# Transposes of 112 rows against transposes of 64 and 48 rows, issued as pairs, in a fused attention and mixer kernel

## The chip, the cores and the metric

The program runs on one core of one Trainium2 chip. The metric is the device time of one launch in microseconds (us); for the kernel before it is the median of three runs, 871.86 us (871.74 to 871.91). The profile is of one further execution of the same program. The engines are called PE (TensorE, the matmuls), PEld (its weight loads), DVE (VectorE), ACT (ScalarE), POOL (GpSimd) and SP (which issues most DMAs).

## The reference, cut to what matters

Three blocks follow one another. All inputs are float32 (the matrices of weights reach the kernel as 64-bit floats and are converted on the chip).

```python
# attention: batch 4, 12 heads, 448 tokens, 64 features to a head
q_n, k_n = rmsnorm(q, g_q), rmsnorm(k, g_k)
attn = softmax(q_n @ k_n.T / 8)                  # 448 x 448 to a head
x = (attn @ v), heads side by side               # (4, 448, 768)
# first mixer: 768 -> 1024, relu, halves u and v
v_n = layernorm(v); v_s = w_spatial @ v_n + b_spatial
x = (u * v_s) @ w_out                            # 512 -> 768
# second mixer: over tokens, then over channels
u = x + relu(x.T @ w_tok1) @ w_tok2 (turned back)
out = u + relu(u @ w_ch1) @ w_ch2
```

## The kernel before, in words

**Tiles.** Two heads are handled together as a pair, 24 pairs in all (NP). The 448 tokens of a pair are cut into four chunks of T = 112 for everything that has tokens on the partitions; P is 128, R is 64, and D, the features of a head, is 64. For each pair q and k are loaded with tokens on the partitions (`load`, line 636), their mean squares are taken (`norms`, line 677: two Square activations on ACT and two row sums on DVE), they are scaled by the roots (`scale`, line 733, on POOL from the third pair on), transposed on PE against an identity matrix so that the features come on the partitions (`transposed`, line 744: four transposes of 112 rows for q, four for k), and copied out of PSUM by ACT, from the ninth pair on with a second half on DVE (line 757 on). `scores` (line 773) multiplies each head of the pair by itself: the contraction is over 64 rows, and the two heads stand in the two halves of the array's rows, so their matmuls are issued two by two. ACT takes the exponentials into a tile `e` of 112 partitions by 2 times 448 columns.

**The turning of the exponentials.** For the product with v the exponentials must have the keys on the partitions. `turned` (line 841) does it for one chunk: seven transposes (ET), each of 112 rows by 128 columns of `e`, the first four into one PSUM bank, the last three into another, and one copy out of each bank, on ACT or (for the second bank of chunks 1 and 3, `ON_DVE`, line 943) on DVE. With 24 pairs and 4 chunks this makes 672 transposes. `values` (line 860) then multiplies with v, 64 output columns to a head, so that the two heads use the two halves of the array's columns. For the first ten pairs (AFTER) the division by the sums is done after that product: `divisors` (line 826) spreads the reciprocals over 64 columns, transposes them (four transposes of 112 rows) and copies the result with one ACT instruction into `over`.

**Order.** Nothing is issued as it is written. Every operation goes into a plan (`Plan.add`, line 159) with a cost from `Plan.estimate` (line 217) and the operations that it depends on, and `place` (line 267) works out an order for every engine: a list schedule by the latest start that a backward pass gives each operation, eight rounds, of which the shortest is kept. For PE the plan holds an attribute `parts`: 0 for a matmul over the whole array, 1 for one of at most 64 rows, 2 for one of at most 64 output columns. Where `parts` changes from one matmul to the next, the plan adds 200 ns (SWITCH, line 346), and it stays with the `parts` that it has while another ready operation of the same `parts` is at most 10,000 ns less urgent (2,500 ns in the first 95 us of plan time; lines 298 to 308, 431). Operations inside `joined_up` (line 211) are issued as one block.

**PSUM.** There are eight banks, of which kind "sc" (scores) owns four, "tp" (transposes) two and "mm" (the mixer's and the values' sums) two (line 133); a kind gets more only where the others' own are not cut into.

**Slots.** `slot` (line 911) lists the work around pair s: loads for s+2, scores of s in four steps, the turning of chunks 2 and 3 of s-1 and 0 and 1 of s, the transposes of q and k of s+1, the values of s-1, the norms of s+2. The mixer's work on the first three batches is merged between the slots and fills PE once the first batch has its six pairs; the fourth batch and the second mixer follow behind.

Of the kernel before, what the change touches and what calls it, by code (L numbers as in the profile page):

```python
# [149 lines left out]
class Plan:  # L150
# [8 lines left out]
    def add(self, engine, fn, args, kwargs):  # L159
# [18 lines left out]
        if engine == "tensor" and fn == "matmul":  # L178
            op.parts = 1 if ins[0].shape[0] <= 64 else 2 if out.shape[0] <= 64 else 0
# [37 lines left out]
    def estimate(self, engine, fn, out, ins, kwargs):  # L217
# [7 lines left out]
        if engine == "tensor":  # L225
            if fn == "transpose":
                return ins[0].shape[0] / 1.2 + 3, 200
# [244 lines left out]
def attention_moe_mixer(  # L472
# [15 lines left out]
    C = 4  # L488
# [137 lines left out]
    class Attention:  # L626
# [9 lines left out]
        def load(self, i):  # L636
            if not 0 <= i < NP:
                return
            b, j = divmod(i, KD)
            t = self.p.tile([T, 2, C, 2, D], F32, tag="raw", bufs=2, name="raw")  # L640

            both = nc.sync if i else nc.scalar

            def load_q(r, on):
                on.dma_start(
                    out=t[:, 0, :, r], in_=q[b, 2 * j + r].rearrange("(c p) d -> p c d", p=T))

            if i:
                load_q(0, nc.sync)
                load_q(1, nc.sync)  # L650
            nc.sync.dma_start(out=t[:, 1, :, 0], in_=k[b, 2 * j].rearrange("(c p) d -> p c d", p=T))

            src = k[b, 2 * j + 1]
            both.dma_start(out=t[:R, 1, 0, 1], in_=src[LAST:])
            both.dma_start(out=t[R:, 1, 0, 1], in_=src[:T - R])
            nc.sync.dma_start(
                out=t[:, 1, 1:, 1], in_=src[T - R:LAST].rearrange("(c p) d -> p c d", p=T))
            if not i:
                load_q(0, nc.sync)
                load_q(1, nc.sync)  # L660
            self.raw[i] = t
            if i == 2:
                self.third = t.tile

# [12 lines left out]
        def norms(self, i, wait=()):  # L677
            if not 0 <= i < NP:
                return
            p, n = self.p, 4 * C  # L680
            raw = self.raw[i].rearrange("p a c r d -> p (a c r) d")
            ss = p.tile([P, n], F32, tag="ss", bufs=3, name="ss")
            for h in (slice(0, n // 2), slice(n // 2, n)):
                sq = p.tile([T, n // 2, D], F32, tag="sq", bufs=1, name="sq")
                sq.tile.after = list(sq.tile.after) + list(wait)
                nc.scalar.activation(sq, raw[:, h], AF.Square)
                nc.vector.reduce_sum(ss[:T, h], sq, axis=AX.X)
            r = rsqrt(p, ss[:T], T, n, 1.0 / D, "r", bufs=3, on=nc.gpsimd if i > 1 else nc.vector)
            self.r[i] = [r[:, :n // 2], r[:, n // 2:]]

        def first(self):
# [3 lines left out]
            raw = self.raw[0].rearrange("p a c r d -> p a (c r) d")  # L695
            self.r[0] = [None, None]

            def squares(a, on):
                sq = p.tile([T, 2, S], F32, tag="e", bufs=EB, name="e").rearrange("p r s -> p (r s)")
                sq = sq[:, :n * D].rearrange("p (n d) -> p n d", d=D)  # L700
                if on is nc.scalar:
                    on.activation(sq, raw[:, a], AF.Square)
                else:
                    on.tensor_tensor(sq, raw[:, a], raw[:, a], op=ALU.mult)
# [15 lines left out]
            self.transposed(0, 0, [known])  # L720
            self.warm(WARM2, [op for _, op in self.qt[0].tile.writers])
            self.transposed(0, 1)
# [10 lines left out]
        def scale(self, i):  # L733
# [4 lines left out]
            for a in range(2) if i else (1,):  # L738
                on = nc.gpsimd if i > 1 else nc.vector
                raw = self.raw[i][:, a].rearrange("p c r d -> p (c r) d")  # L740
                roots = self.r[i][a][:T]
                on.tensor_tensor(raw, raw, roots.unsqueeze(2).to_broadcast([T, 2 * C, D]), op=ALU.mult)

        def transposed(self, i, a, wait=()):
            if not 0 <= i < NP:
                return
            tp = psum.tile([P, C, T], "tp", "tp")
            for c in range(C):
                nc.tensor.transpose(
                    tp[:, c, :], self.raw[i][:, a, c].rearrange("p r d -> p (r d)"), ident[:T, :T])  # L750
            tpf = tp.rearrange("p c t -> p (c t)")
            if i < WHOLE:
                to = self.qt if a == 0 else self.kt
                t = to[i] = self.p.tile([P, S], F32, tag="qt" if a == 0 else "kt", name="whole")
                t.tile.after = list(t.tile.after) + list(wait)
                nc.scalar.activation(t, tpf, AF.Copy, scale=1.0 if a == 0 else self.gg[:, 0:1])
                if a:
# [784 lines left out]
```

## Time and profile before

| what | value |
|---|---|
| median of three runs | 871.86 us |
| span of the profiled execution | 870.8 us |
| time around the span, by the median | 1.06 us |
| PE busy | 854.8 us, 98% |
| DVE, ACT, POOL busy | 684.0, 534.0, 407.9 us |
| the chain that ended last, on PE | 92% |

A line of the profile names an engine, an operation, the tiles that it writes and reads (out<-in) with their partitions and elements, how many there were (x), busy time and the mean of one. In the list in order of time a line merges neighbouring instructions of one kind: start, time from the first one's start to the last one's end, count. A matmul's time has its latency in it, so neighbouring lines overlap, and the pace of a group is read from starts. A transposing matmul stands as `tp<-ident,e 112*128 112x112`: 112 rows by 128 columns are loaded as weights, and the 112 columns of the identity are streamed through them.

### The profile page before, as it was taken

To read this page: it belongs to the slowest core of one execution; us is meant where nothing else is said; L and a number is where in the kernel's file an instruction comes from. 1 tells how busy PE (TensorE), PEld (TensorE's weight loads), DVE (VectorE), ACT (ScalarE), POOL (GpSimd) and SP (SyncE) were. 2 spreads that over 40 slices of the span, in tenths; PEclk is the share of its full clock that TensorE was granted. 3 is DMA by queue.
4 is the path that set the end of the run, shared out by engine and by line. 5 is a ranking of instruction groups with operands and counts; after the bars stand their busy time and mean duration, and the time that the engine had idled before them with its cause. 6 is when DMAs were issued, how large, how long until landed. Compare 5 with 4: busy or idle time off the path is not lost.

```text
span 870.8 us, 15419 instructions
## 1 busy us (share of the span) xinstructions
PE 854.8 (98%) x5000; PEld 721.8 (83%) x5000; DVE 684.0 (79%) x1343; ACT 534.0 (61%) x1278; POOL 407.9 (47%) x538
## 2 busy tenths in 40 slices
PE   6999999999999999999999999999999999999998
PEld 5554567777687787777889999999999999999997
DVE  6889999877886767867476466989889986998963
ACT  6999988788686767766453356655335654343331
POOL 2554746786667636464235223234233108415560
PEclk9999999999999999999999999999999999999999
DMA  7655665467545467444777567876564745752441
GB/s 167 180 134 150 188 182 167 131 198 235 168 120 157 135 198 209 118 144 113 228 260 243 179 219 264 254 238 211 160 164 137 242 123 170 224 167 58 145 153 64
DMA packets 153263, 152.27 MB, mean 175 GB/s; under 512 B 77152, under 2 KB 136352, under 8 KB 153184
## 3 DMA queue, kind: packets, MB, share of 16 engines
q1 hardware_dynamic: 152720, 151.26, 58.7%
q8 instruction: 40, 0.66, 0.3%
q14 instruction: 39, 0.32, 0.1%
q10 hardware_dynamic: 464, 0.03, 0.0%
HBM read 112.44 MB, written 38.80 MB: 174 GB/s over the span
## 4 chain that ended last, share of the span: by engine, by line
PE 92%; ACT 4%; DMA 3%; DVE 1%; issue 0%; SPq 0%; ACTq 0%; POOL 0%; DVEq 0%; POOLq 0%
PE h2ps L424 18%; PE o_ps L424 18%; PE tp L424 10%; PE av L424 8%; PE vps L424 7%; PE ups L424 7%; PE sc L424 7%; PE xps L424 7%; PE sps L424 4%; PE u_ps L424 4%; PE h1ps L424 3%; ACT e L424 2%; DMA raw<-in_moe_w_in_dram 1%; DMA wo<-wo_d 1%; ACT et L424 1%; DMA vrest<-in_v_dram 0%
## 5 line engine op out<-in xcount | busy, mean ns | idle before, releaser
L424 PE MATMUL h2ps<-op,w 128*128 128x448 f32 x756 | 154.2, 366 | 0.0
L424 PE MATMUL o_ps<-w,op 128*128 128x384 f32 x882 | 153.1, 334 | 0.0
L424 PEld LDWEIGHTS o_ps<-w,op 128*128 128x128 f32 x882 | 152.9, 188 | 0.0
L424 PEld LDWEIGHTS h2ps<-op,w 128*128 128x128 f32 x756 | 141.7, 188 | 11.2
L424 ACT ACTIVATE e<-sc,nm 112x448 f32<-112x448 f32 x184 | 119.6, 673 | 24.4 <-DVE nm L424 24.1
L424 DVE TENSOR_REDUCE nm<-sc 112x1 f32<-112x448 f32 x192 | 109.4, 614 | 11.7 <-PE sc L424 11.3
L424 POOL TENSOR_TENSOR src<-src 128x384 f32<-128x384 f32 x48 | 59.2, 1243 | 76.0 <-DMA src<-c_d 62.7
L424 PEld LDWEIGHTS tp<-ident,e 112*128 112x128 f32 x672 | 74.3, 142 | 23.2 <-issue 6.4
L424 ACT ACTIVATE op<-c 128x768 fp32r<-128x768 f32 x49 | 41.5, 847 | 83.6 <-PE o_ps L424 80.2
L424 POOL TENSOR_SCALAR e<-e,sums 112x448 f32<-112x448 f32 x112 | 71.5, 656 | 42.3 <-DVE sums L424 17.1
L424 PE MATMUL tp<-ident,e 112*128 112x112 f32 x672 | 87.5, 263 | 0.4 <-ACT e L424 0.4
L424 ACT ACTIVATE et<-tp 128x448 f32<-128x448 f32 (+1 forms) x144 | 72.6, 544 | 11.7 <-PE tp L424 11.2
L424 DVE SCALAR_TENSOR_TENSOR word<-raw,word 128x256 uint32<-128x256 uint32 (+2 forms) x132 | 70.7, 536 | 1.7
L424 POOL TENSOR_TENSOR u<-u,o 128x384 f32<-128x384 f32 x28 | 41.0, 1483 | 65.7 <-ACT o L424 35.4
L424 DVE TENSOR_SCALAR word<-word 128x256 f32<-128x256 f32 (+5 forms) x132 | 56.7, 437 | 16.9 <-ACT word L424 16.1
L424 DVE TENSOR_TENSOR op<-c,op 128x768 fp32r<-128x768 f32 x49 | 58.7, 1198 | 9.9 <-ACT op L424 9.9
L424 PE MATMUL ups<-xp,wu 128*128 128x448 f32 x288 | 66.1, 373 | 0.0
L424 PE MATMUL av<-et,v 128*64 128x448 f32 x288 | 60.3, 549 | 1.5 <-ACT et L424 1.5
L424 PE MATMUL xps<-wo,g 128*128 128x384 f32 x288 | 59.7, 346 | 1.1 <-DMA wo<-wo_d 1.1
L424 PE MATMUL vps<-wv,xp 128*128 128x512 f32 x216 | 59.2, 408 | 0.0
L424 PEld LDWEIGHTS ups<-xp,wu 128*128 128x128 f32 x288 | 52.6, 188 | 5.0 <-ACT et L424 0.3
L424 DVE TENSOR_TENSOR c<-c,h2ps 128x448 f32<-128x448 f32 x84 | 49.9, 613 | 8.6 <-PE h2ps L424 8.4
(149 smaller groups left out, 1666.5 us busy)
## 6 DMA issues: line engine op xcount, KB each, us to landing
src<-c_d SPq DMA_DIRECT2D x132, 192.0 KB, 3.0
wu<-wu_d SPq DMA_DIRECT2D x16, 768.0 KB, 4.9
wo<-wo_d SPq DMA_DIRECT2D x16, 768.0 KB, 4.8
raw<-in_moe_w_ch_dram SPq DMA_DIRECT2D x36, 256.0 KB, 3.5
raw<-in_moe_w_ch_dram SPq DMA_DIRECT2D x24, 384.0 KB, 3.7
raw<-in_q_dram SPq DMA_DIRECT2D x48, 112.0 KB, 2.8
u<-u_d SPq DMA_DIRECT2D x28, 192.0 KB, 3.9
out_dram<-u SPq DMA_DIRECT2D x28, 192.0 KB, 1.9
```

What stands on the lines that cost most here:

```text
L424: getattr(getattr(self.nc, op.engine), fn)(*args, **kwargs)
```

## The change

The transposes of `e`, of q and k, and of the spread reciprocals are done with at most 64 rows each. A transpose of 112 rows by 128 columns becomes two, one of rows 0 to 63 and one of rows 64 to 111, with 64 and 48 columns of the identity streamed, into two PSUM banks; the two are issued next to each other, and all of a chunk (seven times two) are issued as one block. Copies out of PSUM take a bank each, now split by rows: 7 times 64 and 7 times 48 columns instead of 4 times 112 and 3 times 112. For `over` there are two copies where there was one.

q and k of a pair share one tile of 128 partitions: q has its tokens, 64 at a time, on the lower half, k on the upper, in G = 7 chunks. So `norms` works on 448 columns where it had 512, `scale` has pieces of 512 and 384 where it had two of 512, and there are seven times two transposes where there were eight. The loads of q and k of a pair are five DMAs instead of six. The first pair keeps its old form in two tiles of the `e` ring (`load_first`, `transposed_first`). `parts` is now worked out for transposes as well, and the plan costs a transpose of at most 64 rows at 28 ns.

```diff
-        if engine == "tensor" and fn == "matmul":
+        if engine == "tensor":
             op.parts = 1 if ins[0].shape[0] <= 64 else 2 if out.shape[0] <= 64 else 0
...
             if fn == "transpose":
+                if ins[0].shape[0] <= 64:
+                    return 28, 200
                 return ins[0].shape[0] / 1.2 + 3, 200
...
+            t = self.raw[i] = self.p.tile([P, G, 2, D], F32, tag="raw", bufs=2, name="raw")
+            for r in range(2):
+                nc.sync.dma_start(out=t[:R, :, r], in_=q[b, 2 * j + r].rearrange("(c p) d -> p c d", p=R))
+            nc.sync.dma_start(out=t[R:, :, 0], in_=k[b, 2 * j].rearrange("(c p) d -> p c d", p=R))
             src = k[b, 2 * j + 1]
+            nc.sync.dma_start(out=t[R:, 0, 1], in_=src[LAST:])
+            nc.sync.dma_start(out=t[R:, 1:, 1], in_=src[:LAST].rearrange("(c p) d -> p c d", p=R))
...
+            for cs in (slice(0, G // 2 + 1), slice(G // 2 + 1, G)):
                 on = nc.gpsimd if i > 1 else nc.vector
...
+            tps = [psum.tile([P, G, R], "tp", "tp") for _ in range(2)]
+            raw = self.raw.pop(i).rearrange("p c r d -> p c (r d)")
+            with nc.joined_up():
+                for c in range(G):
+                    for a in range(2):
+                        me = slice(a * R, (a + 1) * R)
+                        nc.tensor.transpose(tps[a][:, c], raw[me, c], ident[me, me])
+            for a in range(2):
+                self.kept(i, a, tps[a].rearrange("p c t -> p (c t)"))
...
-            over = self.over[i] = p.tile([P, S], F32, tag="over", bufs=1, name="over")
-            nc.scalar.activation(over, tp.rearrange("p c t -> p (c t)"), AF.Copy)
+            over = self.over[i] = p.tile([P, C, T], F32, tag="over", bufs=1, name="over")
+            for tp, (t, m) in zip(tps, HALVES):
+                nc.scalar.activation(over[:, :, t:t + m], tp, AF.Copy)
...
-            for h, tiles in enumerate((range(C), range(C, ET))):
-                tp = psum.tile([P, C, T], "tp", "tp")
-                for n in tiles:
-                    t = n // 2 * P + n % 2 * (S + R)
-                    nc.tensor.transpose(tp[:, n - tiles[0], :], e[:, t:t + P], ident[:T, :T])
-                et = self.et[i][:, tiles[0]:tiles[-1] + 1, c * T:(c + 1) * T]
-                tpf = tp[:, :len(tiles)]
+            tps = [psum.tile([P, ET, m], "tp", "tp") for _, m in HALVES]
+            with nc.joined_up():
+                for n in range(ET):
+                    at0 = n // 2 * P + n % 2 * (S + R)
+                    for tp, (t, m) in zip(tps, HALVES):
+                        nc.tensor.transpose(tp[:, n], e[t:t + m, at0:at0 + P], ident[t:t + m, t:t + m])
+            for h, (t, m) in enumerate(HALVES):
+                et = self.et[i][:, :, c * T + t:c * T + t + m]
...
             self.turned(s - 1, 3)
-            self.transposed(s + 1, 0)
+            self.transposed(s + 1)
             yield
             self.scores(s, 1)
             self.normalise(s, 0)
-            self.transposed(s + 1, 1)
             self.values(s - 1)
...
+    G = S // R
+    HALVES = (0, R), (R, T - R)
```

## Rows read from the trace of the kernel before

**Rows 1.** The page: engines over the span, and the chain that ended last.
```profile
PE 854.8 (98%) x5000; PEld 721.8 (83%) x5000; DVE 684.0 (79%) x1343; ACT 534.0 (61%) x1278; POOL 407.9 (47%) x538
...
PE 92%; ACT 4%; DMA 3%; DVE 1%; issue 0%; SPq 0%; ACTq 0%; POOL 0%; DVEq 0%; POOLq 0%
```
**Rows 2.** Busy time by stage: stretch and its length, PE, PEld, DVE, ACT, POOL, clock.
```profile
20.00:100.00 80.00, 76.99 (x461) 41.04 (x459) 70.62 (x157) 77.21 (x220) 45.73 (x74) 0.97 0.60 162
100.00:160.00 60.00, 60.00 (x375) 45.20 (x374) 54.95 (x136) 51.11 (x140) 35.90 (x55) 1.00 0.59 168
160.00:300.00 140.00, 140.00 (x908) 107.06 (x907) 108.78 (x254) 108.01 (x301) 100.30 (x161) 1.00 0.57 165
300.00:436.00 136.00, 136.00 (x858) 106.02 (x857) 91.90 (x236) 89.58 (x240) 66.87 (x108) 1.00 0.58 169
```
**Rows 3.** PE's groups between 100 and 436 us, by shape.
```profile
L424 PE MATMUL tp<-ident,e 112*128 112x112 f32 x504 | 65.2, 259 | 0.0
...
L424 PE MATMUL tp<-ident,raw 112*128 112x112 f32 x128 | 16.0, 260 | 0.0
...
L424 PE MATMUL tp<-ident,wide 112*128 112x112 f32 x16 | 2.2, 262 | 0.0
```
**Rows 4.** PE in order of time: start, time, operation, count.
```profile
123.32 1.07 PE L424 MATMUL vps<-wv,xp 128*128 128x512 f32 x4
124.23 0.83 PE L424 MATMUL tp<-ident,e 112*128 112x112 f32 x7
124.99 1.47 PE L424 MATMUL sc<-kt,qt 64*112 64x448 f32 x12
126.40 2.48 PE L424 MATMUL av<-et,v 128*64 128x448 f32 x12
128.70 0.92 PE L424 MATMUL av<-et,vrest 128*64 128x448 f32 x4
129.55 1.48 PE L424 MATMUL sc<-kt,qt 64*112 64x448 f32 x12
130.97 0.98 PE L424 MATMUL tp<-ident,raw 112*128 112x112 f32 x8
131.72 3.02 PE L424 MATMUL vps<-wv,xr 128*128 128x512 f32 x12
134.58 0.83 PE L424 MATMUL tp<-ident,e 112*128 112x112 f32 x7
135.19 1.47 PE L424 MATMUL ups<-xp,wu 128*128 128x448 f32 x6
136.50 0.83 PE L424 MATMUL tp<-ident,e 112*128 112x112 f32 x7
...
152.30 0.46 PE L424 MATMUL sc<-kt,qt 64*112 64x448 f32 x2
```
**Rows 5.** PE in order of time: two runs of transposes, 112 and 128 columns streamed.
```profile
196.86 1.50 PE L424 MATMUL tp<-ident,e 112*128 112x112 f32 x14
...
511.88 0.82 PE L424 MATMUL tp<-ident,x 128*128 128x128 f32 x6
```
**Rows 6.** PE's group of transposes with 128 columns, whole span.
```profile
L424 PE MATMUL tp<-ident,x 128*128 128x128 f32 x96 | 16.0, 272 | 0.0
```
**Rows 7.** Weight loads in order of time: transposes, a first and its successor; scores.
```profile
156.10 0.14 PEld L424 LDWEIGHTS tp<-ident,e 112*128 112x128 f32 x1 [0.18 <-ACT e L424]
...
156.16 0.24 PEld L424 LDWEIGHTS tp<-ident,e 112*128 112x128 f32 x2
...
152.30 0.17 PEld L424 LDWEIGHTS sc<-kt,qt 64*112 64x112 f32 x2 [0.70 <-DVE wpart L424]
```
**Rows 8.** Copies out of PSUM and work on q and k, by shape, whole span.
```profile
L424 ACT ACTIVATE et<-tp 128x448 f32<-128x448 f32 x96 | 55.2, 577 | 10.9 <-PE tp L424 10.5
...
L424 ACT ACTIVATE sq<-raw 112x512 f32<-112x512 f32 x46 | 30.8, 670 | 0.6 <-DVE ss L424 0.6
L424 ACT ACTIVATE et<-tp 128x336 f32<-128x336 f32 x48 | 23.0, 479 | 0.8 <-PE tp L424 0.7
...
L424 DVE TENSOR_REDUCE nm<-sc 112x1 f32<-112x448 f32 x192 | 109.4, 614 | 11.7 <-PE sc L424 11.3
L424 DVE TENSOR_REDUCE ss<-sq 112x8 f32<-112x512 f32 x46 | 31.3, 680 | 12.1 <-ACT sq L424 12.0
L424 DVE COPY et<-tp 128x336 f32<-128x336 f32 x48 | 24.1, 501 | 22.4 <-PE tp L424 22.3
...
L424 POOL TENSOR_TENSOR raw<-raw,ry 112x512 f32<-112x512 f32 x44 | 47.0, 1083 | 1.3
```
**Rows 9.** DMA issues for q and k: count, KB each, us to landing.
```profile
raw<-in_q_dram SPq DMA_DIRECT2D x48, 112.0 KB, 2.8
...
raw<-in_k_dram SPq DMA_DIRECT2D x24, 84.0 KB, 2.8
...
raw<-in_k_dram SPq DMA_DIRECT2D x23, 12.0 KB, 2.4
```

More of the change, by code (lines that the diff above doesn't have):

```diff
@@ L701, in squares @@
                 if on is nc.scalar:
-                    on.activation(sq, raw[:, a], AF.Square)
+                    on.activation(sq, raw[a], AF.Square)
                 else:
-                    on.tensor_tensor(sq, raw[:, a], raw[:, a], op=ALU.mult)
+                    on.tensor_tensor(sq, raw[a], raw[a], op=ALU.mult)
                 return sq
@@ L735, in scale, with transposed, transposed_first @@
                 return
-            for a in range(2) if i else (1,):
-                on = nc.gpsimd if i > 1 else nc.vector
[L740 to L744, printed above, removed]
+            if not i:
+                raw = self.raw[i][1].rearrange("p c r d -> p (c r) d")
+                roots = self.r[i][1][:T]
+                nc.vector.tensor_tensor(raw, raw, roots.unsqueeze(2).to_broadcast([T, 2 * C, D]), op=ALU.mult)
+                return
+            for cs in (slice(0, G // 2 + 1), slice(G // 2 + 1, G)):
+                on = nc.gpsimd if i > 1 else nc.vector
+                n = 2 * (cs.stop - cs.start)
+                raw = self.raw[i][:, cs].rearrange("p c r d -> p (c r) d")
+                roots = self.r[i][:, 2 * cs.start:2 * cs.stop]
+                on.tensor_tensor(raw, raw, roots.unsqueeze(2).to_broadcast([P, n, D]), op=ALU.mult)
+        def transposed(self, i):
             if not 0 <= i < NP:
                 return
+            tps = [psum.tile([P, G, R], "tp", "tp") for _ in range(2)]
[7 more added lines that the diff above has]
+                self.kept(i, a, tps[a].rearrange("p c t -> p (c t)"))
+            self.r.pop(i)
+        def transposed_first(self, a, wait=()):
             tp = psum.tile([P, C, T], "tp", "tp")
@@ L749, in transposed, with kept @@
                 nc.tensor.transpose(
-                    tp[:, c, :], self.raw[i][:, a, c].rearrange("p r d -> p (r d)"), ident[:T, :T])
-            tpf = tp.rearrange("p c t -> p (c t)")
+                    tp[:, c, :], self.raw[0][a][:, c].rearrange("p r d -> p (r d)"), ident[:T, :T])
+            self.kept(0, a, tp.rearrange("p c t -> p (c t)"), wait)
+            if a:
+                self.raw.pop(0)
+        def kept(self, i, a, tpf, wait=()):
+            to = self.kt if a else self.qt
@@ L877, in values @@
             if i < AFTER:
-                over = self.over.pop(i)
+                over = self.over.pop(i).rearrange("p c t -> p (c t)")
                 nc.vector.tensor_tensor(over, av[:, :S], over, op=ALU.mult)
```

88 lines of the change are left out of this document (39 added, 49 removed).

## The prediction

> **What bounds the kernel now.** I read the page first: PE is busy for 98% of the span and makes 92% of the chain that ended last, where DVE is busy for 79% and ACT for 61% [rows 1]. A busy PE need not be an engine at its limit, so the busy times by stage come next [rows 2]. From 100 to 436 us, where attention and the first mixer run side by side, PE has no idle time at all; DVE comes nearest in the first 60 us of it (55 of 60) and falls to two thirds later, ACT falls from 51 of 60 to 90 of 136. There PE's work is the time. From 20 to 100 us it is otherwise: the mixer has nothing ready, and ACT is busy for 77.2 of 80 us. At most 2.8 us can come out of that stretch, whatever PE saves. After 436 us the transposes that the change touches are over.
>
> So the question is what PE's transposes cost between 100 and 436 us. The groups by shape [rows 3] give 504 of `e`, 128 of q and k, 16 of the reciprocals. At 28 of `e` to a pair these are 18 pairs' work. Their mean of 259 ns is latency; the pace is read from a run of fourteen that takes 1.50 us [rows 5]: (1.50 - 0.259) / 13 = 95.5 ns. A run of six with 128 columns streamed gives (0.82 - 0.272) / 5 = 110 ns [rows 5, 6]. Both are 0.85 to 0.86 ns a column, so the streamed columns set the pace, not the rows.
>
> **What a pair of halves costs.** No row shows a transpose of 64 rows, so it is bounded. Streaming 64 columns takes 64 x 0.853 = 55 ns, and the partner's 48 columns less, if the two run beside each other. The second limit is the weight load, still 128 columns: where nothing held it up, a second load began 0.06 us after the first [rows 7]. If a half's load goes beside its partner's, a pair costs 60 ns, if the loads take turns 120 ns; if only the streams take turns, (64 + 48) x 0.853 = 95.5 ns, as now. The nearest rows are those of the scores, which already run two halves of the rows: two loads lie together in 0.17 us [rows 7], and twelve matmuls of 64 rows take 1.47 us, as do six over the whole array with as many columns each [rows 4]. Both loads and streams run beside each other there. I take 60 ns, and keep 55 and 120.
>
> Then, between 100 and 436 us: for `e` 504 x (95.5 - 60) = 17.9 us; for q and k 128 x 95.5 - 112 x 60 = 5.5 us, seven pairs taking the place of eight transposes; for the reciprocals 16 x 35.5 = 0.6 us. Together 24.0 us off PE, or 1.33 us a pair of heads.
>
> **What it adds on PE: changes between halves and whole.** In the list in order of time [rows 4] a visit to the scores and values has four changes (scores, values, scores, mixer), and a change is visible as a gap: twelve scores have a pace of (1.47 - 0.46) / 5 = 0.20 us a pair, so six pairs need 1.21 us, but the next kind starts 1.41 us after them. A change costs 0.2 us; the plan's SWITCH has the same. The transposes work over the whole array now and are strewn between mixer matmuls at no such price (124.23, 134.58, 136.50). Afterwards each block of transposes that stands alone between mixer matmuls pays two changes, 0.4 us, and saves only 7 x 35.5 = 0.25 us. A block next to scores pays nothing.
>
> The plan knows this and holds on to the kind of work it has. How many blocks can it bring next to scores? A block fills both of the transposes' banks. They are free again when two copies are done: 577 and 479 ns on ACT, or 501 ns on DVE beside ACT's [rows 8], so 0.6 to 1.1 us and the hops, behind whatever ACT has before them. Two blocks in a row would make PE wait; a block, two chunks of scores (1.4 us) and another block would not. A visit of the present form has four such places around its two runs of scores, one for each chunk of `e`. The fifth block, q and k, finds none and costs a visit of its own; and since exponentials come two chunks at a time and five `e` buffers hold them back, I add half a visit for a chunk that isn't ready. One and a half further visits for each of 18 pairs, at 0.4 us, are 10.8 us. The ends: none, and three (21.6 us).
>
> **The rest.** ACT: from the copies, 112 columns are (577 - 479) = 98 ns, 0.88 ns each, with some 185 ns fixed [rows 8]. The second copy of `over` adds 0.19 us for the first ten pairs; squares of 448 in place of 512 columns save 2 x 0.06 us a pair. DVE saves 2 x (680 - 614) = 0.13 us a pair on the sums, POOL a quarter of one scaling of 1083 ns, 0.27 us [rows 8]. These lie beside PE from 100 us on and are costed at nothing there; if PE's cover goes, they are the gain. ACT's copies of `et` have 448 and 336 columns as before, in shorter runs; nothing to a third more is possible, and from 100 us on ACT has room (51 of 60 is the tightest). The first copy now waits until all fourteen halves are done, 7 x 60 = 0.42 us after the block begins where four transposes took 0.38, so nothing is late by it. q's transposes wait for both scalings, up to 1.1 us later than now, in a slot of 336 / 18 = 18.7 us that prepares them one slot ahead: nothing. SP issues five loads where it issued six, the sixth of 2.4 us to landing [rows 9]; the same bytes now go to 64 partitions. The loads run two slots ahead, which covers even a doubling of 2.8 us. Nothing is queued longer on SP.
>
> In the stretch from 20 to 100 us scores, turning and scores alternate, so PE gains more there than anywhere, but ACT is the limit and gets 0.07 us a pair more work. Of the 2.8 us I take 1.0, with ends 0 and 2.8.
>
> **Sum.** 24.0 + 1.0 - 10.8 = 14.2 us. The profiled span is 870.8 us and the median 871.86, so 1.06 us lie around it; I leave them. 871.86 - 14.2 = 857.7 us.
>
> **Rivals.**
>
> *The halves don't keep that pace.* A pair is two loads and two matmuls, four instructions in 60 ns; the scores show four in 0.2 us [rows 4] and no row shows them closer together. If PE starts them no faster than streams in turn would run, a pair costs 95.5 ns, the 24.0 us are gone and the changes stay: 871.9 + 10.8 = 883 us. With loads in turn it is 632 pairs x 120 = 75.8 us against 648 x 95.5 = 61.9: another 13.9 us, 897. For it: nothing shows such a rate. Against it: the concurrency that the scores show. Chance 0.11.
>
> The Trainium skill, TensorE: Matmul & The Clock Gate, section "Wait — 56ns, not 53.3ns?", says that matmuls start at least about 25 ns apart however few their columns are, and the page TensorEngine Tiling (Array Packing), "Instruction Overhead", warns against dividing a dimension that is small already. Two matmuls at that figure are 50 ns and would leave my 60; if it held for the loads too, four would be 100 ns, and the sum would come out as in the rival above. No row here shows which.
>
> *The blocks don't find their places.* This ends slower without any fault of the halves: the place is the change of `parts` around each block, the price 0.4 us, and the two banks are why. If all five blocks of a pair stand alone, 5 x 0.4 = 2.0 us are paid for 1.33: 18 x 0.67 = 12 us slower, 884 us. It decides from 1.33 / 0.4 = 3.3 further visits a pair. For it: today's blocks mostly stand alone [rows 4]. Against: the plan costed them at no change then; now it charges 200 ns each. Chance 0.08.
>
> *Another engine takes over.* The blocks wait for visits, so `e` buffers come free later, scores and exponentials later, and PE meets gaps where it had mixer work; or DVE, at 55 of 60, is the limit from 100 to 160 us. Then some 14 us turn into waits: 871 to 872 us. Against it: PE has no gap now, and DVE's work shrinks too. Chance 0.07.
>
> **How the numbers follow.** The forecast has 0.74, its own range 845 (no further visit, all of the early 2.8) to 868 us (three further visits: 24.0 - 21.6 + 1); pairs at 55 ns would give 3 us more, 842. The range from 843 to 874 holds it and the rival of no change, and leaves out the two slow ones with 0.19. A difference of 0.2%, 1.7 us, is about what a measurement of this kernel can tell from none. Faster 0.74, same 0.07, slower 0.19.
>
> **What would show it.** In the profile after: a block of fourteen halves between two starts at about 0.42 us plus latency, halves of a pair starting together, loads too; transposes next to scores in the order of PE, and some four to seven changes a pair of heads instead of four; PE still without gaps from 100 us on and the end of attention near 422 us instead of 436; ACT as full as now before 100 us. Wrong would be a pace of 95 ns or more for a pair, blocks alone between mixer matmuls five times a pair, or PE waiting for `et` copies.

## The result, and the profile after

The kernel after takes 881.38 us (median of four runs, 880.90 to 883.16), the kernel before beside it 871.80 us: a ratio of 1.011 with an interval of 1.0095 to 1.0124. It is slower by 9.6 us; the prediction said 14.2 us faster, and 881.4 us lies outside its range. The page of the profile after, the engines' shares and the chain that ended last, against [rows 1]:

```profile
PE 843.5 (96%) x5850; PEld 706.5 (80%) x5850; DVE 681.4 (77%) x1343; ACT 533.3 (61%) x1288; POOL 403.5 (46%) x538
...
PE 77%; ACT 10%; DVE 5%; DMA 4%; issue 2%; SPq 2%; POOL 1%; ACTq 0%; DVEq 0%; POOLq 0%
```

PE is busy 11.3 us less than in [rows 1], so work did come off it. But span less busy time, PE's idle time, rose from 870.8 - 854.8 = 16.0 to 881.4 - 843.5 = 37.9 us, and the chain lost its 92% on PE: a tenth of it now runs over ACT. The stages, against [rows 2] (same columns), tell where:

```profile
20.00:100.00 80.00, 65.29 (x609) 35.71 (x609) 67.07 (x144) 70.46 (x202) 41.80 (x70) 0.86 0.57 155
100.00:160.00 60.00, 54.52 (x426) 33.57 (x425) 47.25 (x121) 47.15 (x139) 28.37 (x47) 0.89 0.45 128
160.00:300.00 140.00, 138.44 (x1216) 104.78 (x1217) 110.91 (x264) 110.59 (x309) 98.75 (x162) 1.00 0.61 174
300.00:436.00 136.00, 134.46 (x1155) 105.07 (x1152) 99.21 (x243) 95.32 (x260) 73.85 (x121) 1.00 0.53 156
```

From 160 us on PE is nearly full, as before. Between 20 and 160 us it now idles 20.2 us where it idled 3.0, and ACT, whose 77.2 of 80 us set the pace of the first stage, is at 70.5. No engine is full there any more: they wait for each other. The granted clock, third from the right, is 0.86 and 0.89 where it was 0.97 and 1.00.

When the values of a pair (`av`) start, read off PE in order of time, shows the two effects apart:

| start of, us | before | after | later by |
|---|---|---|---|
| values of the 1st pair | 30.7 | 34.0 | 3.3 |
| values of the 8th pair | 126.4 | 148.5 | 22.1 |
| first mixer matmul of the values (`vps`) | 100.5 | 116.4 | 15.9 |
| values of the 24th pair | 428.1 | 438.6 | 10.5 |

22 us are lost up to the eighth pair, and 301.7 - 290.1 = 11.6 us come back over the other sixteen. What comes back is the forecast's mechanism; what is lost is a stretch that the forecast had costed as a small gain.

**What came as forecast.** PE in order of time, around one visit to scores and values of the kernel after:

```profile
204.83 2.48 PE L426 MATMUL av<-et,v 128*64 128x448 f32 x12
207.14 0.92 PE L426 MATMUL av<-et,vrest 128*64 128x448 f32 x4
207.99 0.64 PE L426 MATMUL tp<-ident,e 64*128 64x64 f32 x14
208.45 1.45 PE L426 MATMUL sc<-kt,qt 64*112 64x448 f32 x12
209.74 0.59 PE L426 MATMUL tp<-ident,e 64*128 64x64 f32 x14
210.25 5.50 PE L426 MATMUL xps<-wo,g 128*128 128x384 f32 x30
```

The block of seven pairs at 209.74 us lasts 0.59 us with a latency of some 0.225 us (the groups below), so a pair takes (0.59 - 0.225) / 6 = 61 ns; the block at 207.99 us, 0.64 us long, gives 69. That is close to the 60 ns that were taken, where a whole transpose had 95.5 [rows 5]. Blocks stand on both sides of the scores, as the plan wanted. PE's groups of the transposes of `e` between 100 and 436 us, against [rows 3]:

```profile
L426 PE MATMUL tp<-ident,e 64*128 64x64 f32 x519 | 46.5, 227 | 0.2 <-ACT over L426 0.2
L426 PE MATMUL tp<-ident,e 48*128 48x48 f32 x519 | 44.9, 225 | 2.2 <-DVE et L426 1.3 <-ACT et L426 0.8
```

The changes of `parts`, counted in the order of PE, rose from 37 to 54 between 160 and 300 us and from 28 to 48 between 300 and 436: by 17 in 7.5 slots and 20 in 7.3, some 2.5 a pair of heads, 1.2 visits where 1.5 were costed.

**What did not.** Between 20 and 130 us, PE's costliest waits before (one line) and after, and the transposes' own wait for copies, that is for a bank, in the view of the waits (engine, what waited, for what; us in total, times, longest):

```profile
PE av L424 <- ACT et L424: 1.5, 3, 0.7
```
```profile
PE tp L426 <- ACT e L426: 9.3, 8, 7.6
PE av L426 <- ACT et L426: 7.4, 5, 2.6
PE av L426 <- ACT e L426: 1.8, 1, 1.8
...
PE tp L426 <- ACT et L426: 1.0, 3, 0.5
```

The same stretch on ACT, before and after:

```profile
ACT et L424 <- PE tp L424: 1.7, 3, 1.2
...
ACT xp L424 <- DVE over L424: 0.5, 2, 0.3
```
```profile
ACT et L426 <- PE tp L426: 5.6, 4, 2.6
ACT xp L426 <- DVE over L426: 4.6, 2, 3.2
```

One wait of the first line after, 7.6 us, is the start, told of below; it began ahead of 20 us, and the kernel before has 4.96 us there. The rest is the circle that follows: the values wait for the copies of the turned exponentials, those copies for the blocks, the blocks for the exponentials, and each engine is idle in turn. The last line closes the circle: `over` is the values' product times the reciprocals, made on DVE, so ACT, which has `xp` to copy from it ahead of its next exponentials, stands waiting for the values themselves, 4.6 us where it was 0.5. One turn of the circle in order of time, PE first (from the values of the pair before, with two blocks in a row at 82.38 us and four later values behind it), then ACT; the time in brackets is the wait ahead:

```profile
60.48 2.48 PE L426 MATMUL av<-et,v 128*64 128x448 f32 x12 [1.75 <-ACT e L426]
...
70.39 0.64 PE L426 MATMUL tp<-ident,e 48*128 48x48 f32 x13 [0.17 <-ACT e L426]
...
71.62 0.65 PE L426 MATMUL tp<-ident,raw 64*128 64x64 f32 x13 [0.33 <-ACT e L426]
74.06 4.75 PE L426 MATMUL av<-et,v 128*64 128x448 f32 x12 [1.79 <-ACT et L426]
...
82.38 1.04 PE L426 MATMUL tp<-ident,e 64*128 64x64 f32 x28
...
92.58 3.60 PE L426 MATMUL av<-et,v 128*64 128x448 f32 x12 [2.65 <-ACT et L426]
...
108.33 4.75 PE L426 MATMUL av<-et,v 128*64 128x448 f32 x12 [1.77 <-ACT et L426]
...
127.70 4.17 PE L426 MATMUL av<-et,v 128*64 128x448 f32 x12 [0.75 <-ACT et L426]
...
148.55 4.07 PE L426 MATMUL av<-et,v 128*64 128x448 f32 x12 [1.45 <-ACT et L426]
```
```profile
71.41 0.94 ACT L426 ACTIVATE et<-tp 128x448 f32<-128x448 f32 x2
72.16 0.71 ACT L426 ACTIVATE e<-sc,nm 112x448 f32<-112x448 f32 x1
...
72.77 0.71 ACT L426 ACTIVATE e<-sc,nm 112x448 f32<-112x448 f32 x1
...
73.38 0.63 ACT L426 ACTIVATE et<-tp 128x448 f32<-128x448 f32 x1
```

PE is through with the blocks by 72.3 us, but the last copy stands behind two more exponentials on ACT and ends at 74.0; the values begin then. They also take 4.75 us for twelve, and the later ones 3.60 to 4.75, where the undisturbed ones at 204.83 took 2.48. The granted clock was lower there (busy times by stretch, columns as in [rows 2], kernel after):

```profile
18.70:28.90 10.20, 6.62 (x60) 4.42 (x62) 7.69 (x20) 8.31 (x24) 6.36 (x12) 0.50 0.54 113
73.30:80.10 6.80, 6.04 (x18) 2.15 (x20) 4.09 (x10) 4.61 (x13) 2.24 (x4) 0.50 0.66 177
```

There, and in five more stretches up to 152 us (from 46.0, 93.8, 107.4, 127.9 and 148.4 us on), TensorE runs at 1.2 instead of 2.4 GHz, 37.5 us in all. The five from 73.3 us on each lie within 1.3 us of the start of values that had waited for `et`, the five of the fence. The kernel before has one such stretch ahead of its last microsecond or two:

```profile
17.75:24.60 6.85, 5.56 (x24) 4.00 (x25) 5.20 (x13) 5.82 (x17) 2.91 (x6) 0.50 0.59 137
```

**The start.** SP's queue, before and after:

```profile
6.54 1.38 SPq L424 DMA_DIRECT2D raw<-in_moe_w_in_dram  x3
10.17 0.89 SPq L424 DMA_DIRECT2D raw<-in_q_dram  x2
```
```profile
7.28 1.27 SPq L426 DMA_DIRECT2D raw<-in_q_dram  x2
8.60 1.97 SPq L426 DMA_DIRECT2D raw<-in_k_dram  x3
10.61 1.06 SPq L426 DMA_DIRECT2D raw<-in_moe_w_in_dram  x2
```

The first pair's q and k now lie in the ring of `e`, so both `raw` buffers are free for the second and third pair, and SP issues the third pair's loads at 7.28 us, ahead of the mixer's weights; before, they went out at 10.17, behind them. ACT stands in front of the first exponential until the weights land:

```profile
12.70 0.67 ACT L424 ACTIVATE word<-raw 128x512 f32<-128x512 f32 x1 [0.62 <-DMA raw<-in_moe_w_in_dram]
13.27 0.71 ACT L424 ACTIVATE e<-sc,nm,r0y 112x448 f32<-112x448 f32 x1
```
```profile
15.91 0.66 ACT L426 ACTIVATE word<-raw 128x512 f32<-128x512 f32 x1 [2.91 <-DMA raw<-in_moe_w_in_dram]
16.48 0.71 ACT L426 ACTIVATE e<-sc,nm,r0y 112x448 f32<-112x448 f32 x1
```

That is 3.2 us, and the first values are late by 3.3.

So three theories stand beside each other for the 22 us: the **start** (order of the loads), the **form** (fourteen halves in one block that holds both banks, with both copies behind its end), and the **clock**.

Two more things go with them. The form also changes what the values wait for: a values matmul reads one turned tile over all 448 tokens, so with copies split by rows it needs both copies of every chunk, where the first half of a pair's values needed only the copies of the first bank. And every kernel below has a new **plan**, worked out anew for all engines. What a plan alone moves can be read off `e_only8` (last group), which leaves loads and forms of the first eight pairs as they were: its first values start at 33.4 us, its seventh pair's at 113.6 and its eighth's at 135.5, against 30.7, 110.1 and 126.4 in the kernel before (twelve scores and eight transposes more lie ahead of the last, some 2 us of its 9.1 by [rows 4], an estimate). So differences of some 5 us between two single plans are not proof of a cause by themselves.

### The profile page after: what moved, and what is told of

The parts are those of the page before. It is cut to its first block, busy times and chain, and to the rows that moved or that the text cites. A ratio compares the mean times of both kernels' runs of the same rounds, so it can differ in the third digit from the quotient of the medians.

```text
span 881.4 us, 17062 instructions
## 1 busy us (share of the span) xinstructions
PE 843.5 (96%) x5850; PEld 706.5 (80%) x5850; DVE 681.4 (77%) x1343; ACT 533.3 (61%) x1288; POOL 403.5 (46%) x538
## 4 chain that ended last, share of the span: by engine, by line
PE 77%; ACT 10%; DVE 5%; DMA 4%; issue 2%; SPq 2%; POOL 1%; ACTq 0%; DVEq 0%; POOLq 0%
PE o_ps L426 17%; PE h2ps L426 17%; PE av L426 8%; PE xps L426 7%; PE ups L426 6%; PE tp L426 5%; PE sc L426 4%; PE vps L426 4%; PE sps L426 4%; ACT e L426 4%; PE h1ps L426 3%; PE u_ps L426 2%; ACT et L426 2%; SPq L426 2%; DMA raw<-in_k_dram 1%
## 5 line engine op out<-in xcount | busy, mean ns | idle before, releaser
L426 PEld LDWEIGHTS h2ps<-op,w 128*128 128x128 f32 x756 | 141.7, 188 | 11.7 <-DVE op L426 0.8
L426 ACT ACTIVATE e<-sc,nm 112x448 f32<-112x448 f32 x184 | 117.3, 655 | 9.2 <-DVE nm L426 8.8
L426 POOL TENSOR_TENSOR src<-src 128x384 f32<-128x384 f32 x48 | 61.2, 1283 | 74.3 <-DMA src<-c_d 41.8
L426 POOL TENSOR_SCALAR e<-e,sums 112x448 f32<-112x448 f32 x112 | 72.2, 661 | 31.8 <-DVE sums L426 22.3
L426 ACT ACTIVATE et<-tp 128x448 f32<-128x448 f32 x144 | 69.6, 525 | 23.3 <-PE tp L426 22.9
L426 PEld LDWEIGHTS tp<-ident,e 64*128 64x128 f32 (+1 forms) x1344 | 54.4, 140 | 35.6 <-issue 10.7
L426 PE MATMUL av<-et,v 128*64 128x448 f32 x288 | 69.9, 627 | 11.4 <-ACT et L426 9.5
L426 DVE SCALAR_TENSOR_TENSOR word<-raw,word 128x256 uint32<-128x256 uint32 (+2 forms) x132 | 77.7, 589 | 1.9
L426 PE MATMUL tp<-ident,e 48*128 48x48 f32 (+1 forms) x1344 | 62.6, 228 | 3.5 <-DVE et L426 1.3
L426 DVE TENSOR_SCALAR word<-word 128x256 uint32<-128x256 uint32 (+5 forms) x132 | 54.3, 417 | 11.9 <-ACT word L426 9.8
L426 PE MATMUL xps<-wo,g 128*128 128x384 f32 x288 | 55.7, 341 | 0.1
L426 PEld LDWEIGHTS av<-et,v 128*64 128x64 f32 x288 | 21.4, 153 | 42.4 <-issue 29.2
```

The source lines that it names most:

```text
L426: getattr(getattr(self.nc, op.engine), fn)(*args, **kwargs)
```

## The experiments

All times are medians beside the kernel before on the same chip (872.0 to 872.4 us). "Time at 1.2 GHz" is worked out from the mean granted clock c of a run's span, 2 x (1 - c) x span, as a mean over the runs; by this the kernel before has 7 us and the one after 39.

**third: the old place of the third pair's loads in the queue.**

```diff
+            if i == 2:
+                t.tile.after = [u for x in self.pair0 for u in x.tile.users]
...
+            self.pair0 = tq, tk
```

> The changed kernel, with one wait put back: the load of q and k of the third pair waits until the first pair's q and k have been transposed, as it did when the first pair took one of the two raw buffers. Theory start: the loss before 20 us (first exponentials at 16.5 us in place of 13.3, behind an ACT wait of 2.9 us for the load of w_in, which SP now issues behind the third pair's loads) comes from that; first exponentials back at 13.3 us and 3 us off the time, 878 us. Theories clock and order (below) alone: the start comes back, but the time stays at 880 to 882 us, since the loss up to 150 us is made elsewhere.

Measured 874.70 us (872.21 to 876.70, ten runs; ratio 1.0026, 1.0012 to 1.0039): 6.7 us faster than after, more than either theory had. But the first exponential came only 0.85 us sooner, for the weights still landed late:

```profile
14.97 0.66 ACT L426 ACTIVATE word<-raw 128x512 f32<-128x512 f32 x1 [2.10 <-DMA raw<-in_moe_w_in_dram]
...
15.63 0.71 ACT L426 ACTIVATE e<-sc,nm,r0y 112x448 f32<-112x448 f32 x1
```

The other 5.8 us are not the wait itself. The plan is worked out anew with the added dependence, and the time at 1.2 GHz fell to 27.6 us; how much each has of it stays open. The later experiments keep this edit, unless they say otherwise.

**fill: keep PE busy in its waits.** To the kernel after, matmuls of the identity by itself are added on PE, eight ahead of the first eight pairs' values and three ahead of each of their blocks; the plan doesn't know of them.

```diff
+            if i < FILL:
+                nc.fill[nc.ops[-1]] = tps[0].rearrange("p n m -> p (n m)")[:, :P], ident, 3
...
+                if i < FILL and not kc:
+                    nc.fill[nc.ops[-1]] = av[:, :P], ident, 8
```

> The changed kernel with the same plan and order, plus idle work for PE: for the first eight pairs eight matmuls of the identity with itself are issued just before the first values matmul, and three before each block of halves of e, into the bank that the block then overwrites. Nothing else differs. Theory clock: PE does so little in the first 150 us that its clock is granted at 1.2 GHz in seven stretches (31 us more than before), and the values, which everything waits for, run at half pace (4.8 us in place of 3.16): the fillers keep the clock at 2.4 GHz, the values take 3.2 us, and 9 to 13 us come off: 868 to 872 us. Theory order: the loss is waits that the new order of blocks makes, and the clock only shows them; the clock may rise, but the time stays at 879 us or more, and the fillers cost up to 3 us.

891.73 us (ratio 1.0227, 1.0210 to 1.0244), far above what either theory gave. The clock held (0.96 and 1.00 in the first two stages of the table by stage, against 0.86 and 0.89); the filling is the likely trouble. PE in order of time:

```profile
49.94 2.05 PE L425 MATMUL av<-ident 128*128 128x128 f32 x16
...
55.08 0.94 PE L425 MATMUL tp<-ident 128*128 128x128 f32 x6
```

One filling matmul is two instructions here (eight show as sixteen), so eight cost 2.0 us and three 0.87, some 5.5 us a pair, and they ran where PE had no wait as well. It tells that a full clock alone doesn't bring the time back if it must be bought with PE's time, and no more.

**third_fill4: the same, cheaper.** `third` with four such matmuls ahead of the first eight pairs' values alone.

> The kernel with the third pair's load waiting (third), with four matmuls of the identity issued just before the first values matmul of the first eight pairs, into the bank that the values overwrite; about 1 us a pair, where PE now waits 0.4 to 2.0 us for copies. Plan and order are the same. Theory clock: the clock no longer falls in those waits, values take 3.2 us throughout, and the time falls to 867 to 872 us. Theory order: 874 to 878 us whatever the clock does.

871.26 us (869.63 to 877.21, ten runs; 0.9999, 0.9983 to 1.0014), 18.3 us at 1.2 GHz in place of 27.6. So 9.3 us less of the low clock go with 3.4 us less time, 0.37 us for each, net of the filling. Between the runs of one kernel time goes with the clock too: of the eleven kernels with six to ten runs, nine have slopes of 0.23 to 0.52 us for 1 us at 1.2 GHz, two (`same_order`, `e_only8`) hardly any. Taken at 0.3, the 32 us that the kernel after has more would be near 10 us (an estimate), and they are not independent of the waits.

**whole_e and whole_third: the first eight pairs' exponentials and divisors whole again.** As before the change, in blocks of four and three with a copy behind each; `whole_e` is the kernel after with this edit, `whole_third` has the edit of `third` too.

```diff
+            if i < FROM:
+                for h, tiles in enumerate((range(C), range(C, ET))):
+                    tp = psum.tile([P, C, T], "tp", "tp")
+                    for n in tiles:
+                        t = n // 2 * P + n % 2 * (S + R)
+                        nc.tensor.transpose(tp[:, n - tiles[0], :], e[:, t:t + P], ident[:T, :T])
...
+    FROM = 8
```

> The changed kernel, but for the first eight pairs e and the reciprocals are transposed as before, 112 rows at once in blocks of four and three; q and k keep their halves. Theories clock and order both: the loss up to 150 us (22 us at the eighth pair's values, of which about 3 from the start) goes but for the 3 us, and the gain behind it (11.6 us from the eighth pair's values to the last's) stays: 861 to 866 us. If only the start were at fault: 880 us or more.

> Both of the edits: e and reciprocals of the first eight pairs whole, and the third pair's load waiting. If the causes add up, 3 us less than the kernel with the first eight pairs whole alone: 858 to 863 us, faster than both kernels. Theory that the start is hidden later by ACT: the same time as without the wait.

870.91 us (868.85 to 873.37; 0.9990, 0.9978 to 1.0001) and 863.84 us (863.37 to 866.91; 0.9914, 0.9894 to 0.9933). Ten to eleven microseconds come back with the old form (and the plan that goes with it), with or without `third`, and with both the change is worth 8 us instead of costing 10. `whole_e` had been expected at 861 to 866 us. PE's waits of `whole_third` between 20 and 130 us, one of ACT's, and its first two stages (the profiled execution is the slowest of the four, 866.91 us):

```profile
PE av L426 <- ACT et L426: 1.6, 3, 0.8
```
```profile
ACT xp L426 <- DVE over L426: 1.0, 1, 1.0
```
```profile
20.00:100.00 80.00, 75.51 (x492) 38.60 (x490) 70.81 (x152) 76.23 (x218) 44.70 (x73) 0.96 0.56 147
100.00:160.00 60.00, 58.78 (x436) 41.07 (x433) 55.25 (x138) 52.75 (x150) 35.24 (x54) 1.00 0.60 175
```

ACT is full again (76.2 of 80), the values wait as little as before the change, and the eighth pair's start at 129.9 us.

What of the form is it: PE's work, the plan's grouping by kind, or the block? Four kernels were made to part these.

**same_order: whole transposes in the halves' order.** `third`, with the instructions of the early blocks of `e` whole, but cost, kind and dependences as told to the plan left as they were, so that every engine keeps the order of `third`.

```diff
+                    if i < FROM:
+                        nc.tensor.transpose(tps[n // C][:, n % C], e[:, at0:at0 + P], ident[:T, :T])
+                        continue
...
+            nc.ops[-1].cost, nc.ops[-1].parts = 28 * 2 * ET, 1
```

> The kernel with the third pair's load waiting (third), and for the first eight pairs e is transposed 112 rows at once, but the plan is given the same costs, kinds and dependences as for the halves, so every engine issues the same work in the same order; the copies out of PSUM have the old shapes, of the same sizes. Only what PE does inside a block differs. Theory clock: seven transposes of 112 rows keep PE busier than fourteen halves, the stretches at 1.2 GHz after 27 us (13.6 us in all) go or shrink, and the time falls from 874.7 to 866 to 871 us although each block is 0.24 us longer and has two more changes of kind. Theory order (blocks of fourteen with two banks, copies that the values wait for): the order is the same, so the time stays at 874 us or rises to 880.

872.03 us (0.9999, 0.9989 to 1.0010): between the two theories, 2.7 us better than `third`, of the 10.9 that `whole_third` brings. PE is busy 842.3 us here against 834.9 in `third`, 7.4 us more, and the kernel is no slower by it: PE's time isn't what the early stretch is short of. Most of the loss, 8.2 us, stays with the order and with what it is made from: blocks of fourteen, two banks, copies behind the end, values that need every copy.

**wt_parts: the grouping.** `whole_third`, but the early whole transposes told to the plan as matmuls of halves (`parts` 1).

> As the kernel with the first eight pairs whole and the third pair's load waiting (863.84 us), with the same blocks of four and three in a bank each, but the plan is told that these whole transposes are of the kind of the scores (64 rows), so it brings them together with the scores as it does with halves. Theory grouping: that the plan groups them makes the values wait and ACT run dry, and the time rises to 869 to 873 us, as in the kernel of the halves' order (872.03). Theory block: grouping costs nothing, 862 to 866 us.

869.14 us (864.47 to 873.44; 0.9967, 0.9948 to 0.9986), 5.3 us slower than `whole_third`, with a wide scatter. That is no more than what a plan alone moves, so a part of grouping in the loss is possible and not shown.

**third_near0: the reach of the grouping.** `third` with `NEAR` 0 in place of 2500: in the first 95 us of plan time PE stays with its kind only among equals.

> The kernel of halves with the third pair's load waiting (874.7 us), and the plan's reach for work of the same kind set from 2,500 to 0 ns in its first 95 us (one constant). Theory grouping: values and scores come when they are due, PE waits less for copies, and the time falls to 866 to 871 us. Theory block: 873 to 877 us.

876.67 us (1.0047, 1.0033 to 1.0061), no better than `third`. It does not test the grouping, though: between 20 and 100 us PE's order has 18 changes of `parts` in this kernel and 18 in `third` (before: 58), so the halves still stand with the scores.

**wt_block: the block.** `whole_third`, but the seven whole transposes of a chunk are one joined block into both banks and both copies stand behind its end. Kind and cost stay those of whole transposes.

> As the kernel with the first eight pairs whole and the third pair's load waiting (863.84 us), but the seven whole transposes of a chunk are one block that takes both of the transposes' banks at once and is copied out behind its end, as the halves must be; kind and cost in the plan are those of whole transposes. Theory block: a block needs both banks free and both copies go behind its end, so ACT, which sets the pace up to 100 us, and PE wait for each other: 868 to 872 us. Theory grouping: 862 to 866 us.

875.76 us (873.27 to 877.38; 1.0042, 1.0029 to 1.0054): 11.9 us slower than `whole_third`, with no half of `e` in those pairs. Its waits of PE and of ACT between 20 and 130 us, and its first two stages:

```profile
PE av L426 <- ACT et L426: 12.6, 7, 2.7
```
```profile
ACT xp L426 <- DVE over L426: 6.3, 2, 3.2
```
```profile
20.00:100.00 80.00, 70.78 (x447) 36.93 (x446) 68.52 (x155) 73.88 (x210) 46.66 (x74) 0.93 0.64 167
100.00:160.00 60.00, 54.88 (x370) 36.95 (x370) 48.95 (x125) 47.23 (x137) 31.97 (x51) 0.94 0.54 154
```

The picture of the kernel after stands again: the values waiting for `et` (1.6 us in `whole_third`), ACT and PE both with gaps, the clock low (22.3 us at 1.2 GHz against 8.2). PE's order has 56 changes of `parts` between 20 and 100 us, nearly as many as before the change, and the copies are split as before, so neither grouping nor the split by rows is needed: a block, both banks at once and copies only behind its end, makes the wait. Which of the two it is, this run does not part.

**wt6 and wt11: where the halves begin to pay.** `whole_third` with the halves from the 7th and from the 12th pair.

> As the kernel with the first eight pairs whole and the third pair's load waiting (863.84 us), but only six pairs whole, so that the halves begin where the mixer starts. If halves cost nothing once the mixer fills PE, 861 to 863 us; if ACT still sets the pace there, 865 to 868 us.

> As the kernel with the first eight pairs whole and the third pair's load waiting (863.84 us), but eleven pairs whole. Each further pair gives up the 0.6 us that a pair of heads gained behind 126 us (11.6 us over 16 to 17 pairs): 865 to 867 us. If pairs nine to eleven lose with halves (in the kernel with eight whole the ninth pair's values come 6 us later than before): 859 to 862 us.

870.46 us (0.9990, 0.9974 to 1.0006) and 863.44 us (863.08 to 865.28; 0.9904, 0.9889 to 0.9919). From the seventh pair is too early (6.6 us slower than from the ninth, outside both forecasts), from the twelfth as good as from the ninth. `wt11` is the fastest version measured, 8.8 us under the kernel before beside it (872.20).

**qk_only, e_only8 and e_only11: what each kind of halves earns.** `qk_only` is `whole_third` with exponentials and divisors whole for all pairs. The other two are the kernel before with halves of `e` alone, from the 9th and from the 12th pair.

```diff
-    FROM = 8
+    FROM = 24
```

> e and the reciprocals of all 24 pairs are transposed whole, as before the change; q and k keep their halves and their shared tile, and the third pair's load waits. Against the kernel in which the first eight pairs alone are whole (863.84 us) this shows what the halves of e bring behind the eighth pair: by the pace in the trace of the changed kernel (62 ns a pair of halves) and one further visit a pair of heads, 16 x (28 x 33.5 ns - 0.4 us) = 8.6 us, so 870 to 874 us. If the changes between kinds eat the gain: 862 to 866 us.

> The kernel before, with halves for e alone and from the ninth pair on; q, k, reciprocals, loads and the first eight pairs as before. Theory that q and k earn as forecast (some 16 x 0.35 us, 5.5 us): this kernel lacks that, and gains only the 9.0 us of e, less nothing for the early stretch: 863 us, or up to 866 us if the halves of q and k also help the plan to fill its visits. Theory that q and k give back by their early loads, scalings and clock what they earn behind (only q and k: 873.65 us, 1.6 us slower than before): 860 to 863 us, the fastest of all.

> As the kernel before with halves for e alone, from the twelfth pair on. Three pairs fewer have halves: 3 x 0.56 us (9.0 us over 16 pairs) slower than from the ninth pair on, so 1.7 us more, if the gain a pair is even; the same or less if the ninth to eleventh pairs, where DVE was busiest, gain nothing.

873.65 us (1.0015, 1.0001 to 1.0028), 869.70 us (0.9971, 0.9959 to 0.9983) and 870.86 us (0.9982, 0.9970 to 0.9993). Against `whole_third`, dropping the halves of `e` costs 9.8 us (PE's busy time: 852.7 against 842.0, 10.7 us), dropping those of q and k 5.9 us (847.2 against 842.0, 5.2 us). A part of these differences is the plan's: with the same early forms of `e` the eighth values start at 129.9 us in `whole_third`, at 135.5 in `e_only8` and at 133.4 in `qk_only`. And the two kinds don't add up: beside the kernel before, halves of q and k alone cost 1.6 us and halves of `e` alone earn 2.7, where both together earn 8.2. PE's busy time is the safer measure, though it too grows where the clock is low: against the 854.8 us before it is 2.1 us less with q and k alone, 7.6 with `e` alone and 12.8 with both. So each kind takes work off PE, `e` the most, but `e_only8` is slower than both theories had it, and how much of each reaches the time depends on what stands beside it.

## Why the prediction was wrong

**The pace of a pair** was right: 61 to 69 ns against 60. The rival in which the halves don't keep pace is out. One step towards it did not follow: the two runs of [rows 5] have as many rows as streamed columns, 112 and 128, so they could not show that the columns and not the rows set the pace. Of the Trainium skill's page TensorE: Matmul & The Clock Gate, section "Wait — 56ns, not 53.3ns?", the prediction asked whether its 25 ns between starts holds for loads too: it does not here, since a pair's four instructions fit in 61 ns, 15 ns each.

**The mixer's stretch** was right in its mechanism. Forecast were 24.0 us off PE less 10.8 for further visits over 18 pairs, 11.7 us over 16; 11.6 us came back between the 8th and the 24th pair's values. That they agree so closely is luck in part: there were 1.2 further visits a pair where 1.5 were costed, but PE also idled 3.1 us between 160 and 436 us, where the forecast had no gap. The rival in which blocks don't find their places is out. Beside `whole_third`, the halves of `e` from the ninth pair earn 9.8 us net and those of q and k 5.9; beside the kernel before they earn 2.7 and lose 1.6, so these are no prices of the two kinds by themselves.

**The early stretch** is the step that failed: "Of the 2.8 us I take 1.0, with ends 0 and 2.8". It took ACT's 77.2 of 80 us for a bound that can only be approached. ACT was full because its copies and exponentials nearly always found something ready, and the change took that away: 70.5 of 80 us. So the term had no end on the slow side, against what was done for every other unknown cost; by the 8th pair's values 22 us were lost, 3.3 of them ahead of the first values. The prediction had named "PE waiting for `et` copies" as a sign of being wrong; that sign came, 7.4 us for 1.5.

**The sentence inside it** that was wrong: "The first copy now waits until all fourteen halves are done ... so nothing is late by it". It compared 0.42 us with 0.38 us of PE's time. What mattered was not how long a block lasts, but what it holds: two banks from its start and two copies until its end. Four transposes needed one bank, and the copy of one bank could run while the other was filled. With the blocks joined and the plan made anew, `wt_block` shows 11.9 us, and PE's wait of the values for `et` at 12.6 us for 1.6. Of the two, the copies are what the waits show; a bank is hardly waited for (1.0 us in all after the change, for `et` ahead of a transpose), though the plan may have put the blocks later on account of the banks. "Two blocks in a row would make PE wait" did not come so either: at 82.38 us PE runs two blocks, 28 halves, in 1.04 us without a wait. The prediction used the banks only to count places in the mixer's stretch, where PE had mixer matmuls to do meanwhile; the early stretch has none. The Trainium skill's page TensorEngine Tiling (Array Packing), "Gotcha 1: PSUM Pressure", says that row tiling raises the pressure on PSUM because different row tiles write to different banks. The kernel after has it so, two banks to a block; what `wt_block` prices is the whole block with whole transposes, and no run shows the price of the banks alone.

**"Nothing is queued longer on SP"** was wrong at the start: it looked at the number of loads and their bytes, not at when their buffers come free. `third` gives 6.7 us against after and `whole_third` 7.1 against `whole_e`; only 0.9 us of it is seen at the first exponential, and the rest, new order and less time at 1.2 GHz, was not separated.

**The clock** was in no term, since before the change it was at 1.0 from 24.6 us on. With the waits it fell.

The rival "another engine takes over" named gaps on PE from blocks and buffers, but from 100 us on and at most down to no change; it is the nearest to what came, mostly in the wrong stage (14.7 us of PE's idle time lie between 20 and 100 us, 5.5 between 100 and 160) and with too small a price.

The balance, in one line of each profiled execution: the span grew by 881.4 - 870.8 = 10.6 us, which is 21.9 us more idle time on PE less 11.3 us less busy time, and that busy time still holds matmuls stretched over 30 us more at 1.2 GHz. The causes overlap (form with its plan 10.9 or 10.5, start with its plan 6.7 or 7.1, clock some 10 inside both, an estimate), so they don't add up to a sum. Open besides: how much of each is the plan's alone, whether both halves of a block could share a bank, or each half be copied before its partner block ends; none of it was tried.

## What to carry to other kernels

Cost a change stage by stage, with both signs in each: where an engine off the saved path is full only because others feed it in time, ask what the new form holds and for how long (banks, buffers, the point from which its reader can begin), not only how long it runs. Here, joining work into a larger block cost little where the waiting engine had other work and much where it had none, so look for the point from which the new form pays and try several: from the seventh pair, where the mixer's work begins, was too early, from the ninth or the twelfth pair, with the third pair's load put back, it turned 10 us slower into 8 us faster. When a buffer moves to another pool, look at what can now be issued earlier, and what that stands in front of.

## What the runs showed of the hardware

Two transposes in the two halves of the rows, with their loads, sustain a pair in 61 to 69 ns; in the records of the block at 209.74 us the two of a pair start 1 to 11 ns apart, and their weight loads 1 to 8. That is closer than the 25 ns of the Trainium skill's page named above, so between two row halves that distance doesn't hold; over a block it is 30 to 34 ns a matmul on average.

The granted clock fell to 1.2 GHz beside single waits of PE of 0.75 to 2.65 us (the five stretches from 73.3 us on); twelve values matmuls then take up to 4.75 us for 2.48. Not every such wait brought a fall: after the one of 1.75 us ahead of the values at 60.48 us the clock stayed at 2.4 GHz until 73.3. One kernel's runs differ in how much: `third` has 20.9 to 31.5 us at 1.2 GHz and takes 872.2 to 876.7 us, and its time goes with it (0.24 us for 1 us); which of the two moves the other, no run shows.
